# Converting weights two steps ahead in a fused Fourier-mixing and ELU-MLP kernel

## The chip, the cores and the metric

One core of one Trainium2 chip. The metric is the device time of one execution in microseconds (us). All executions quoted are of the fast state. "Before" is the kernel as it was; "the changed kernel" has the change. Most kernels repeat within 0.3% on one chip. Before does not quite: in the sets of the experiments, 48 of its 54 executions took 1976.0 to 1980.9 us and six took 1982.8 to 1987.7. Where another kernel fell in two groups, they are told. "Slow clock" is the time that matmuls lose when TensorE's granted clock has dropped: the trace grants 0.57 of full speed from 112.4 to 115.7 us in before.

## The reference

```python
X = np.fft.fft(np.fft.fft(x, axis=1), axis=2).real.astype(np.float32)      # x: 8 x 3008 x 256, float32
h = X.reshape(24064, 256) @ w_in                        # w_in: 256 x 2048, float64
g = np.where(h > 0, h, np.exp(np.minimum(h, 0)) - 1)
out = (g @ w_out).astype(np.float32)                    # w_out: 2048 x 256, float64
```

Both weights come in as 64-bit floats and are converted on the core, by integer and float work on VectorE, ScalarE and GpSimd.

## The kernel before

TensorE carries the kernel: discrete Fourier transforms as matmuls, the channel transform folded into w_in, then per step of some 5.2 us two blocks of hidden units of one tile of 256 columns. In steps 0 to 15 the first two tiles alternate, so chunk c of w_in (256 hidden units) is first used in step 2c, and chunk c of w_out, which multiplies what came of those hidden units, in step 2c+2. Meanwhile the weights are still being converted. The program gives every piece of work a time on an ideal clock (`T` is one step, 4.8 us on that clock) and emits it in that order; `pin` keeps that order on its engine. What is not pinned, the DMAs above all, a scheduler may move.

```python
# conversion of a chunk: fields (VectorE), power (ScalarE), round and scale (GpSimd, VectorE)
for chunk, k in ((w2_chunks[0], 0), (w1_chunks[2], 1), (w1_chunks[3], 2), (w2_chunks[1], 3),
                 (w1_chunks[4], 4), (w2_chunks[2], 5), ..., (w1_chunks[7], 10),
                 (w2_chunks[5], 11), (w2_chunks[6], 12), (w2_chunks[7], 14)):   # w1 = w_in, w2 = w_out
    ...
# fold of w_in chunk c on TensorE, its copy on ScalarE, its last row to a column by two DMAs
def spread_last_row(q):
    c = slice(q * 256, (q + 1) * 256)
    queue = nc.sync if q else nc.gpsimd
    queue.dma_start(out=wx_dr[:, c], in_=Ws[127:128, c])          # to DRAM
    queue.dma_start(out=wex[:, 2 * q : 2 * q + 2],                 # back as a column
                    in_=wx_dr[:, c].rearrange("o (f p) -> p (o f)", p=128))
# even part on VectorE needs that column:  E = Rb * wex + H
# sums of w_out for later steps, GpSimd
for i in range(8):
    at((11 + 0.7 * i) * T + 1.0, lambda i=i: sum_weights(i))
# loads of one batch of x; two of four go by index, from GpSimd
def load_x(b):
    for j in (2, 1):
        nc.gpsimd.indirect_dma_start(out=L[j], in_=xflat, ...)
    nc.sync.dma_start(out=L[3], ...); nc.sync.dma_start(out=L[0], ...)
    if b == NB - 1:                                                # last batch: one row again
        nc.gpsimd.dma_start(out=L[1][0:1, 0 : 5 * ND], in_=xrows(b, SEQ - 5, 1, 1, 5))
# element-wise loads of one channel of x for all batches (4-byte elements), SyncE
for n in range(16):
    at((13 + 0.7 * n) * T, lambda: load_ext(...))
```

Of the kernel before, what the change touches and what calls it, by code (L numbers as in the profile page):

```python
# [11 lines left out]
U32 = mybir.dt.uint32  # L12
# [5 lines left out]
SEQ = 3008  # L18
ND = 256
NDFF = 2048  # L20
NF = NDFF // 128
HALF = SEQ // 2
# [68 lines left out]
def kernel(  # L91
# [7 lines left out]
    nc = tc.nc  # L99
# [19 lines left out]
    pin = tc.keep_in_program_order  # L119
# [12 lines left out]
    xflat = x.rearrange("b s d -> (b s) d")  # L132
    ix = cpool.tile([128, 3], I32, tag="ix")
# [16 lines left out]
    def load_x(b):  # L150
        L = [
            spool.tile([128, 6 * ND], FP, tag=f"xl{j}", bufs=1, name=f"xl{j}")
            for j in range(4)
        ]
        for j in (2, 1):
            c = 1 if j == 2 else 2 if b == NB - 1 else 0
            nc.gpsimd.indirect_dma_start(
                out=L[j],
                out_offset=None,
                in_=xflat,  # L160
                in_offset=bass.IndirectOffsetOnAxis(
                    ap=ix[:, c : c + 1].bitcast(U32), axis=0
                ),
                element_offset=b * SEQ * ND,
            )
        nc.sync.dma_start(out=L[3], in_=xrows(b, HALF, 6, 128))
        nc.sync.dma_start(out=L[0], in_=xrows(b, 0, 6, 128))
        if b == NB - 1:
            nc.gpsimd.dma_start(
                out=L[1][0:1, 0 : 5 * ND], in_=xrows(b, SEQ - 5, 1, 1, 5)  # L170
            )
        return L
# [5 lines left out]
    Ws = cpool.tile([128, NDFF], FP, tag="Ws")  # L178
# [115 lines left out]
    def w1_dst(c):  # L294
# [6 lines left out]
    IN_HOMES = [(f"WT{c}", 1, 1024) for c in range(4)] + [  # L301
        Wc[:, 1024:2048],
        ("WT0", 1, 1024),
        ("WT1", 1, 1024),
        ("WT2", 1, 1024),
    ]
    OUT_HOMES = [w2[:, 1024 * (c + 1) : 1024 * (c + 2)] for c in range(3)] + [
        ("WT3", 1, 1024),
        ("WT0", 1, 1024),
        ("rx", 1, HALF + 1),  # L310
        ("ot", 2, 1024),
        ("ot", 2, 1024),
# [84 lines left out]
    def fold_chunk(c):  # L397


        ps = folds[c] = bank("H")  # L400
        chunk = w1_chunks[c]
        dst = chunk.dst()
        for n in range(2):
            cols = slice(256 * n, 256 * n + 256)
            for h in range(1 if chunk.pairs else 2):
                for half in range(2):
                    odd = n == half
                    block = 2 * odd + half + 2 * (odd and h)
                    mm(
                        ps[64 * half : 64 * half + 64, cols],  # L410
                        CC[:, 64 * block : 64 * block + 64],
                        chunk.ab[:, 256 * odd : 256 * odd + 256]
                        if chunk.pairs
                        else dst[:, h],
                        n == 0 and h == 0,
                        h == 1 or chunk.pairs,
                    )
# [5 lines left out]

    def spread_last_row(q):
        c = slice(q * 256, (q + 1) * 256)
        queue = nc.sync if q else nc.gpsimd
        queue.dma_start(out=wx_dr[:, c], in_=Ws[127:128, c])
        with nc.allow_non_contiguous_dma(reason="one row to columns"):
            queue.dma_start(
                out=wex[:, 2 * q : 2 * q + 2],  # L430
                in_=wx_dr[:, c].rearrange("o (f p) -> p (o f)", p=128),
            )


    def turn_last_row(q):

        for j in range(2):
            f = 2 * q + j
            mm(
                folds[q][:, j : j + 1],  # L440
                Ws[:, f * 128 : (f + 1) * 128],
                pick[:, 32:33],
                True,
            )

    def put_last_row(q):
        act(wex[:, 2 * q : 2 * q + 2], folds[q][:, 0:2])
# [4 lines left out]
    def sum_weights(i):  # L452
        if not WT:
            for j in range(4):
                WT.append(
                    spool.tile([128, 8, 128], FP, tag=f"WT{j}", bufs=1, name=f"WT{j}")
                )
        b11, b12 = w2v[:, 2 * i, 0:128], w2v[:, 2 * i, 128:256]
        b21, b22 = w2v[:, 2 * i + 1, 0:128], w2v[:, 2 * i + 1, 128:256]
        W = [t[:, i] for t in WT]  # L460
        gtt(W[2], b12, b22, ALU.add)
        gtt(W[1], b11, W[2], ALU.subtract)
        gtt(W[0], b12, b11, ALU.subtract)
        gtt(W[3], W[1], b21, ALU.add)
# [212 lines left out]
    def ext_side(g, rows=NB):  # L677
        n = NO if g > 1 else NE
        t = spool.tile([128, NE], FP, tag="bs", bufs=2, name="bs")
        act(t[0:rows, 0:n], state["ext"][32 * g : 32 * g + rows, 0:n])  # L680
        state["side", g] = t[0:rows, 0:n]
# [392 lines left out]
    def at(t, fn):  # L1074
        events.append((t, len(events), fn))
# [32 lines left out]

    at(-13.1, lambda: dft_now(state["x_even"], 1, "pC"))
    at(-13.1, lambda: dft_now(state["x_even"], 0, "pD"))  # L1110
    at(-13.05, lambda: spread_last_row(0))
    at(-11.5, lambda: state["x_even"].copy())
    at(-11.0, lambda: fold_now("o0 o1 O0 EO2"))
    at(-10.95, R_even.copy)
# [13 lines left out]
    T = PERIOD  # L1128
    for chunk, k in (
        (w2_chunks[0], 0),  # L1130
        (w1_chunks[2], 1),
        (w1_chunks[3], 2),
        (w2_chunks[1], 3),
        (w1_chunks[4], 4),
        (w2_chunks[2], 5),
        (w1_chunks[5], 6),
        (w2_chunks[3], 7),
        (w1_chunks[6], 8),
        (w2_chunks[4], 9),
        (w1_chunks[7], 10),  # L1140
        (w2_chunks[5], 11),
        (w2_chunks[6], 12),
        (w2_chunks[7], 14),
    ):
        t = k * T
        first = (
            (0.96, 0.96, 0.97, 1.9),
            (2.1, 2.9, 2.91, 4.22),
            (2.95, 2.96, 2.97, 4.2),
            (0.95, 0.96, 0.97, 4.2),  # L1150
        )
        dt = first[k] if k < 4 else (-0.5, 0.05, 0.06, 2.95)
        for d, fn in zip(dt, (chunk.fields, chunk.power, chunk.round, chunk.scale)):
            at(t + d, fn)
    for chunk, t in (
        (w1_chunks[6], 0.95),
        (w1_chunks[7], 2.2),
        (w2_chunks[3], 3.2),
        (w2_chunks[4], 7.1),
        (w2_chunks[6], 8.3),  # L1160
        (w2_chunks[7], 12.2),
    ):
        at(t * T, chunk.load)
    for c in range(1, 8):
        t = max(2 * c - 3, c % 3) * T + 4.7 if c > 1 else 2.3
        at(t, lambda c=c: fold_chunk(c))
        t = max(2 * c - 2, 3) * T + 0.03 if c > 1 else 3.0
        at(t, lambda c=c: put_chunk(c))
        if c > 1:
            at(t + 0.01, lambda c=c: spread_last_row(c))  # L1170
    at(3.15, lambda: turn_last_row(1))
    at(T + 0.25, lambda: put_last_row(1))
    for i in range(8):
        at((11 + 0.7 * i) * T + 1.0, lambda i=i: sum_weights(i))
    at(2 * T + 4.2, lambda: fold_now("EO3"))
    total = n_tiles * 8
    WINOGRAD = (
# [75 lines left out]
    def at_half(step, d, par, col):  # L1253
        assert step + 1 >= safe(col)
        t = step * T

        def run():
            d().ps = bank("H")
            d().mms(par, d().ps)

        at(t + 4.75, run)
        if par:
            at(t + T + 1.46, lambda: d().copy())
        else:
            at(t + T + 1.01, lambda: d().plus())
            at(t + T + 1.02, lambda: d().minus())
# [16 lines left out]
    for t, fn in (  # L1283
# [7 lines left out]
        (T + 4.21, R_odd.minus),  # L1291
    ):
        at(t, fn)
    at_half(4, lambda: I_odd, 1, 0)
    at_half(6, lambda: I_odd, 0, HALF)
    at(10 * T + 4.75, dft_ext_0)
    for g in (2, 3):
        at(11 * T + 1.46, lambda g=g: ext_side(g, 1))
    at(12 * T + 1.35, lambda: ext_rows(1, gtt, 1))
    at(12 * T + 2.0, lambda: spread_ext(0, 1))  # L1300
    for n in range(16):
        j, k = divmod(n, 4)
        at(
# [13 lines left out]
    for b in range(1, NB):  # L1317
        s0 = (b - 1) * steps_b
        l0 = s0 - 8 if b > 1 else 5.2
        at(l0 * T + 0.1, lambda b=b: state.update(L=load_x(b)))  # L1320
        f0, f1 = (s0 - 1, s0 + 38) if b > 1 else (8, 37)
        at(f0 * T, lambda b=b: begin_folds(b))
        n = 0
        for key in fold_keys:
            at(
                int(f0 + n * (f1 - f0) / n_big) * T + 1.3,
                lambda key=key: state["ops"][key](),
            )
            n += key[0][0] not in "cx"
        for n, (ri, kodd) in enumerate(((0, 0), (1, 0), (0, 1), (1, 1))):  # L1330
            at_dft(
                s0 + (28, 34, 38, 42)[n], 2, b, ri, kodd,
                lambda k=2 * ri + kodd: state["EO"][k],
            )
        for kodd in range(2):
            step = s0 + (28, 38)[kodd]
            assert step >= safe(b * HALF + (kodd + 1) * RUN)
            at(step * T + 1.0, lambda b=b, kodd=kodd: spread_ext(b, kodd))
# [50 lines left out]
```

## Time and profile before

| | before |
|---|---|
| time, median of the first 3 runs | 1979.11 us (1977.59 to 1979.69) |
| span of the profiled run | 1975.6 us |
| TensorE busy | 1956.9 us |
| waits of TensorE on w_out (steps 4, 10, 12) | 0.95, 1.80, 3.90 us |

TensorE is busy 99% of the span. So the time is its work, plus its idle times, plus what a lowered clock costs after some of them. The prediction shows the lines.

### The profile page before, as it was taken

The page shows a single profiled execution, that of the slowest core. Times are in us where ns is not written, and L with a number is a line of the kernel's source. Part 1 is how long each engine was busy: PE and PEld are TensorE (multiplying, and loading weights), DVE is VectorE, ACT ScalarE, POOL GpSimd, SP SyncE. Part 2 cuts the span into 40 slices and gives each one's busy share as a digit, 9 for nine tenths or more (in the row PEclk, how much of TensorE's full clock was granted, in tenths as well). Part 3 has the DMA queues.
Part 4 walks back from the last instruction along what each step waited for, and adds up shares of the span by engine and source line. Part 5 has one row for each costly group of instructions (what it writes and reads, how often), then busy time and mean ns, then how long its engine had stood idle before and what let it go on. Part 6 is the DMA issues. An engine that isn't in the chain of part 4 may idle for free.

```text
span 1975.6 us, 26860 instructions
## 1 busy us (share of the span) xinstructions
PE 1956.9 (99%) x8908; PEld 1656.1 (84%) x8908; DVE 1275.2 (65%) x2325; ACT 869.0 (44%) x1667; POOL 1361.8 (69%) x1802
## 2 busy tenths in 40 slices
PE   9999999999999999999999999999999999999998
PEld 5778888888888888888888888888888888888887
DVE  8856566666667666666566665666556765666666
ACT  4644434444344444444344443444444444344443
POOL 4678758786587766777567875678657776455665
PEclk9999999999999999999999999999999999999999
DMA  9156101121001110121100211013010110100101
GB/s 354 33 21 88 39 13 19 33 60 24 12 19 43 46 29 11 18 54 37 26 18 13 65 26 26 12 19 89 7 21 11 20 22 14 16 12 12 22 9 24
DMA packets 255610, 71.02 MB, mean 36 GB/s; under 512 B 243998, under 2 KB 244914, under 8 KB 255088
## 3 DMA queue, kind: packets, MB, share of 16 engines
q1 hardware_dynamic: 250896, 56.46, 14.9%
q0 software_dynamic: 2400, 12.59, 1.9%
q8 instruction: 70, 1.15, 0.2%
q14 instruction: 68, 0.56, 0.1%
q10 hardware_dynamic: 2176, 0.26, 0.1%
HBM read 44.43 MB, written 24.80 MB: 35 GB/s over the span
## 4 chain that ended last, share of the span: by engine, by line
PE 96%; DVE 2%; POOL 1%; issue 0%; ACT 0%; POOLq 0%; DVEq 0%
PE H L380 38%; PE pD L380 16%; PE pC L380 16%; PE pB L380 16%; PE pA L380 8%; PE M L380 1%; POOL G L389 0%; DVE E L759 0%; POOL w L389 0%; DVE pow L279 0%; DVE G L785 0%; DVE v L386 0%; DVE pow L225 0%; DVE w L231 0%; DVE Ir L386 0%
## 5 line engine op out<-in xcount | busy, mean ns | idle before, releaser
L389 POOL TENSOR_TENSOR G<-G 128x256 f32<-128x256 f32 x1440 | 1034.7, 728 | 549.2 <-DVE G L785 438.9
L759 DVE SCALAR_TENSOR_TENSOR E<-Rb,wex,H 128x256 f32<-128x256 f32 x752 | 327.9, 477 | 613.0 <-PE H L380 608.1
L392 ACT ACTIVATE G<-H 128x512 f32<-128x512 f32 x376 | 224.5, 597 | 958.6 <-DVE G L769 955.9
L380 PE MATMUL H<-Ir,Ws 128*128 128x256 f32 x1504 | 387.6, 380 | 1.5 <-DVE E L759 1.0
L380 PE MATMUL H<-Rr,Wc 128*128 128x256 f32 x1504 | 387.0, 380 | 0.0
L380 PE MATMUL pC<-G,WT 128*128 128x256 f32 x1440 | 369.6, 379 | 0.0
L380 PEld LDWEIGHTS H<-Rr,Wc 128*128 128x128 f32 x1504 | 284.6, 190 | 56.0 <-issue 4.1
L380 PEld LDWEIGHTS H<-Ir,Ws 128*128 128x128 f32 x1504 | 277.8, 189 | 51.0 <-DVE E L759 3.9
L380 PEld LDWEIGHTS pC<-G,WT 128*128 128x128 f32 x1440 | 273.6, 190 | 37.2
L769 DVE SCALAR_TENSOR_TENSOR G<-E,H 128x512 f32<-128x512 f32 x376 | 257.1, 684 | 44.5 <-PE H L380 8.5
L785 DVE SCALAR_TENSOR_TENSOR G<-G,H 128x512 f32<-128x512 f32 x376 | 255.9, 681 | 24.8 <-ACT G L392 24.8
L785 DVE SCALAR_TENSOR_TENSOR G<-M,G 128x512 f32<-128x512 f32 x376 | 256.9, 683 | 0.0
L380 PE MATMUL pA<-G,w 128*128 128x256 f32 x784 | 231.0, 382 | 6.6 <-POOL w L389 6.6
L392 ACT ACTIVATE G<-G 128x512 f32<-128x512 f32 x376 | 233.3, 620 | 0.0
L380 PE MATMUL pB<-G,w 128*128 128x256 f32 x784 | 229.3, 379 | 0.0
L380 PE MATMUL pD<-G,w 128*128 128x256 f32 x784 | 229.3, 379 | 0.0
L392 ACT ACTIVATE M<-G 128x512 f32<-128x512 f32 x376 | 224.2, 596 | 0.0
L392 ACT ACTIVATE M<-M 128x512 f32<-128x512 f32 x376 | 220.9, 588 | 0.0
L380 PE MATMUL pD<-G,WT 128*128 128x256 f32 x720 | 214.4, 379 | 1.6 <-DVE v L386 1.6
L380 PE MATMUL pB<-G,WT 128*128 128x256 f32 x720 | 214.6, 380 | 0.7 <-POOL G L389 0.6
L380 PEld LDWEIGHTS pA<-G,w 128*128 128x128 f32 x784 | 149.5, 191 | 28.3 <-POOL w L389 7.9
L380 PEld LDWEIGHTS pB<-G,w 128*128 128x128 f32 x784 | 149.0, 190 | 20.2
(137 smaller groups left out, 1401.7 us busy)
## 6 DMA issues: line engine op xcount, KB each, us to landing
out_dram<-ot SPq DMA_DIRECT2D x496, 32.0 KB
xl<-in_x_dram SPq DMA_DIRECT2D x16, 768.0 KB
out_dram<-ot SPq DMA_DIRECT2D x256, 2.0 KB
Rb<-r SPq DMA_DIRECT2D x10, 376.0 KB
raw<-in_moe_w_in_dram SPq DMA_DIRECT2D x7, 512.0 KB
MC<-dft_mats SPq DMA_DIRECT2D x3, 1131.0 KB
raw<-in_moe_w_out_dram SPq DMA_DIRECT2D x5, 512.0 KB
out_dram<-ot SPq DMA_DIRECT2D x64, 28.0 KB
```

The costliest lines, as they stand in the source:

```text
L380: nc.tensor.matmul(out_, lhsT=lhsT, rhs=rhs, start=start, stop=stop, skip_group_check=True)
L389: pin(nc.gpsimd.tensor_tensor(out=o, in0=a, in1=b, op=op))
L392: pin(nc.scalar.activation(out=o, in_=i, func=func, **kw))
L759: nc.vector.scalar_tensor_tensor(out=S.E[:, c], in0=Rb[:, cols(i)], scalar=wex[:, f : f + 1], in1=S.H[:, c], op0=ALU.mult, op1=ALU.add,)
L769: nc.vector.scalar_tensor_tensor(out=two(S.G[:, 0:512])[:, :, ::-1], in0=two(S.E), scalar=2.0, in1=two(S.H), op0=ALU.mult, op1=ALU.subtract,)
L785: nc.vector.scalar_tensor_tensor(out=o, in0=e, scalar=-1.0, in1=h, op0=ALU.add, op1=ALU.max)
```

## The change

The intent: convert every chunk of w_out two steps ahead of its use, in even steps, and w_in in odd ones; put pieces of folding x behind the conversions in GpSimd's order; sum the weights later; make the first weight column with two small matmuls, not two DMAs. Buffers are exchanged to suit. The core of the diff:

```diff
-            nc.gpsimd.indirect_dma_start(
-                out=L[j],
+            pin(
+                nc.gpsimd.indirect_dma_start(
+                    out=L[j],
...
-        queue = nc.sync if q else nc.gpsimd
+        queue = nc.sync
...
-        (w1_chunks[3], 2),
-        (w2_chunks[1], 3),
-        (w1_chunks[4], 4),
-        (w2_chunks[2], 5),
+        (w2_chunks[1], 2),
+        (w1_chunks[3], 3),
+        (w2_chunks[2], 4),
+        (w1_chunks[4], 5),
...                                      # and so on to (w2_chunks[5], 10), (w1_chunks[7], 11)
-        t = max(2 * c - 3, c % 3) * T + 4.7 if c > 1 else 2.3
-        at(t, lambda c=c: fold_chunk(c))
-        t = max(2 * c - 2, 3) * T + 0.03 if c > 1 else 3.0
+        at((2 * c - 2) * T + 4.7 if c > 1 else 2.3, lambda c=c: fold_chunk(c))
+        t = (2 * c - 1) * T + 0.03 if c > 1 else 3.0
...
-    at(-13.05, lambda: spread_last_row(0))
+    at(-10.6, lambda: turn_last_row(0))
+    at(-10.59, lambda: put_last_row(0))
...
-        at((11 + 0.7 * i) * T + 1.0, lambda i=i: sum_weights(i))
+        at((13 + 0.6 * i) * T + 3.6, lambda i=i: sum_weights(i))
...                                      # some transforms one step earlier, homes of chunks
-                int(f0 + n * (f1 - f0) / n_big) * T + 1.3,
+                slot * T + (3.5 if slot < 16 else 1.3),
```

More of the change, by code (lines that the diff above doesn't have):

```diff
@@ L156, in load_x @@
             c = 1 if j == 2 else 2 if b == NB - 1 else 0
-            nc.gpsimd.indirect_dma_start(
-                out=L[j],
-                out_offset=None,
-                in_=xflat,
-                in_offset=bass.IndirectOffsetOnAxis(
-                    ap=ix[:, c : c + 1].bitcast(U32), axis=0
-                ),
-                element_offset=b * SEQ * ND,
+            pin(
+                nc.gpsimd.indirect_dma_start(
+                    out=L[j],
+                    out_offset=None,
+                    in_=xflat,
+                    in_offset=bass.IndirectOffsetOnAxis(
+                        ap=ix[:, c : c + 1].bitcast(U32), axis=0
+                    ),
+                    element_offset=b * SEQ * ND,
+                )
             )
@@ L303 @@
         ("WT0", 1, 1024),
-        ("WT1", 1, 1024),
+        ("WT3", 1, 1024),
         ("WT2", 1, 1024),
@@ L307 @@
     OUT_HOMES = [w2[:, 1024 * (c + 1) : 1024 * (c + 2)] for c in range(3)] + [
-        ("WT3", 1, 1024),
-        ("WT0", 1, 1024),
+        Ws[:, 1024:2048],
+        ("WT1", 1, 1024),
         ("rx", 1, HALF + 1),
@@ L1131 @@
         (w1_chunks[2], 1),
-        (w1_chunks[3], 2),
-        (w2_chunks[1], 3),
-        (w1_chunks[4], 4),
-        (w2_chunks[2], 5),
-        (w1_chunks[5], 6),
-        (w2_chunks[3], 7),
-        (w1_chunks[6], 8),
-        (w2_chunks[4], 9),
-        (w1_chunks[7], 10),
-        (w2_chunks[5], 11),
+        (w2_chunks[1], 2),
+        (w1_chunks[3], 3),
+        (w2_chunks[2], 4),
+        (w1_chunks[4], 5),
+        (w2_chunks[3], 6),
+        (w1_chunks[5], 7),
+        (w2_chunks[4], 8),
+        (w1_chunks[6], 9),
+        (w2_chunks[5], 10),
+        (w1_chunks[7], 11),
         (w2_chunks[6], 12),
@@ L1155 @@
     for chunk, t in (
-        (w1_chunks[6], 0.95),
-        (w1_chunks[7], 2.2),
-        (w2_chunks[3], 3.2),
-        (w2_chunks[4], 7.1),
+        (w2_chunks[3], 0.5),
+        (w2_chunks[4], 0.95),
+        (w1_chunks[7], 3.2),
+        (w1_chunks[6], 5.1),
         (w2_chunks[6], 8.3),
@@ L1293 @@
         at(t, fn)
-    at_half(4, lambda: I_odd, 1, 0)
-    at_half(6, lambda: I_odd, 0, HALF)
-    at(10 * T + 4.75, dft_ext_0)
+    at_half(3, lambda: I_odd, 1, 0)
+    at_half(5, lambda: I_odd, 0, HALF)
+    at(9 * T + 4.75, dft_ext_0)
     for g in (2, 3):
-        at(11 * T + 1.46, lambda g=g: ext_side(g, 1))
-    at(12 * T + 1.35, lambda: ext_rows(1, gtt, 1))
-    at(12 * T + 2.0, lambda: spread_ext(0, 1))
+        at(10 * T + 1.46, lambda g=g: ext_side(g, 1))
+    at(11 * T + 3.55, lambda: ext_rows(1, gtt, 1))
+    at(11 * T + 3.6, lambda: spread_ext(0, 1))
     for n in range(16):
@@ L1324 @@
         for key in fold_keys:
+            slot = int(f0 + n * (f1 - f0) / n_big)
             at(
-                int(f0 + n * (f1 - f0) / n_big) * T + 1.3,
+                slot * T + (3.5 if slot < 16 else 1.3),
                 lambda key=key: state["ops"][key](),
```

## The prediction

> **What bounds the kernel now.** I read the page first (busy shares, chain), then what TensorE waited for, then the timelines of TensorE, GpSimd, VectorE and the DMA queue of SyncE over the first 150 us, since every edited line acts there or only shifts an issue later on.
>
> ```profile
> PE 1956.9 (99%) x8908; PEld 1656.1 (84%) x8908; DVE 1275.2 (65%) x2325; ACT 869.0 (44%) x1667; POOL 1361.8 (69%) x1802
> PE 96%; DVE 2%; POOL 1%; issue 0%; ACT 0%; POOLq 0%; DVEq 0%
> ```
>
> TensorE is busy 1956.9 of 1975.6 us and is 96% of the chain that ended last. So no change that leaves its matmuls alone can win more than the 18.7 us of idle time plus what a lowered clock cost. Of those 18.7 us, 1.1 lie before the first matmul and some 6 after the last one. The rest is a handful of waits (timeline of TensorE: start, us, then in brackets the idle time before and what ended it):
>
> ```profile
> 40.99 1.13 PE L380 MATMUL H<-Ir,Ws 128*128 128x256 f32 x4 [0.95 <-DVE E L759]
> 53.42 1.99 PE L380 MATMUL pA<-G,w 128*128 128x256 f32 x8 [0.95 <-POOL w L389]
> 90.53 1.08 PE L380 MATMUL H<-raw,CC 128*64 128x256 f32 x8 [0.40 <-POOL raw L389]
> 94.47 1.99 PE L380 MATMUL pA<-G,w 128*128 128x256 f32 x8 [1.80 <-POOL w L389]
> 112.40 3.37 PE L380 MATMUL pA<-G,w 128*128 128x256 f32 x8 [3.90 <-POOL w L389]
> 115.56 1.39 PE L380 MATMUL H<-Ir,Ws 128*128 128x256 f32 x4
> 116.78 1.89 PE L380 MATMUL pB<-G,w 128*128 128x256 f32 x8
> ```
>
> The three waits on "POOL w" are matmuls of steps 4, 10 and 12, each the first to need a freshly converted chunk of w_out, whose last multiply GpSimd had not done. The last is the dearest, and slow afterwards: eight matmuls in 3.37 us against 1.89, four in 1.39 against 1.03, so 1.84 us lost to the clock (0.83 granted in the slice from 110 to 120 us). GpSimd shows why it was late:
>
> ```profile
> 102.00 1.29 POOL L389 TENSOR_TENSOR w<-raw,w 128x512 f32<-128x512 f32 x1 [1.75 <-ACT w L392]
> 107.60 0.46 POOL L389 TENSOR_TENSOR WT<-w 128x128 f32<-128x128 f32 x1 [4.31 <-PE H L380]
> ...
> 109.51 1.17 POOL L473 TENSOR_TENSOR e<-xl 128x384 f32<-128x384 f32 x1
> 110.64 1.71 POOL L389 TENSOR_TENSOR w<-w,pow 128x512 f32<-128x512 f32 x1
> ```
>
> The multiply at 110.64 had its operand from VectorE at 104.8. But a weight sum (WT) stood ahead of it in GpSimd's order; its buffer was still the raw home of the last w_in chunk, free only after that chunk's fold matmuls (107.4). Then a fold of x followed. The wait is order, not load.
>
> **What the Trainium skill says.** "TensorE: Matmul & The Clock Gate", first table: the queues of ScalarE, VectorE and GpSimdE are strict FIFO. The trace agrees: 4.31 us of idle GpSimd with a ready multiply behind. The same page, "Why this matters for your kernels": TensorE idle for more than about 3 us falls back to half clock. The trace agrees: after 3.90 us idle, the 1.84 us above; after 1.80 us idle, none. "DMA: Bandwidth & Descriptors", "Queues, rings and completion order": on each DMA engine the descriptors of a ring are consumed in ring order, and SyncE has one row of rings. No wait of before depends on that, but the change will.
>
> **The change part by part.**
> Conversions: w_out chunk c moves from step 2c+1 to step 2c, where its first matmul comes in step 2c+2. In before the multiply ended 5 to 6 us after the first matmul of its step where nothing stood ahead of it (step 5: 59.74 to 64.92; step 7: 73.21 to 79.27). Two steps are at least 10.4 us of TensorE, so the new slack is some 5 us. The three waits go: 0.95+1.80+3.90, and 1.84 of slow clock.
> w_in chunk c moves to step 2c-3 and its fold from step 2c-3 to step 2c-2. The conversion-to-fold distance stays; the x fold pieces that stood before the pairs (84.46 to 87.1) now stand behind, so the 0.40 goes. Sum so far: 0.95+0.40+1.80+3.90+1.84 = 8.9 us.
> First weight column: two more matmuls with one output column (0.36 us in the same job of the next column), and a 0.16 us copy, in place of two DMAs from GpSimd. The VectorE row of step 0 may start 1.6 us earlier (28.61 now), but the one of step 1 waits for matmuls that end 0.36 us later. VectorE is then busy without a gap to 59.7, so the wait of 0.95 at 40.99 stays and swallows both. Zero.
> Later batches: both indirect loads of x become neighbours in GpSimd's order, between the third and fourth sum of a step, with no fold beside them. 2 x 1.02 us delay the fourth sum, which has over 3 us until TensorE uses it (334.6 against 338.0 in a quiet step). No cost; the one wait they caused before (0.59 us at 196.6) goes. Gain 0.6.
> Weight sums: start at step 13.75 instead of 11.2 and must be done in step 18. GpSimd then has some 26 us of work for five steps of 5.2: just enough.
>
> **What it adds: a late column.** The fold of w_in now ends one step before use, not two. Its last row must still go Ws to DRAM to wex by two DMAs on SyncE's queue before VectorE may start the even part of step 2c. When the queue is free this is cheap:
>
> ```profile
> 107.90 0.24 SPq L427 DMA_DIRECT2D wx<-Ws  x1
> 109.03 0.36 SPq L429 DMA_DIRECT2D wex<-wx  x1
> 118.38 0.24 SPq L703 DMA_DIRECT2D r<-rx  x1
> 119.56 0.34 SPq L710 DMA_DIRECT2D Rb<-r  x1
> 119.95 0.29 SPq L714 DMA_DIRECT2D Ir<-r  x1
> 120.28 15.11 SPq L609 DMA_DIRECT2D x<-in_x_dram  x8
> ```
>
> 1.1 us between the two issues, an estimated 2 us to land: about 3.5 in all, against one step of 5.2 us plus 1. It fits for chunks 2 to 6. For chunk 7 it does not. In before its two DMAs preceded the element-wise loads of x. In the built order of the changed kernel SyncE has: the three DMAs of r, one x load, wx of chunk 7, three x loads of 1536 elements, one of 8, then wex of chunk 7. And the even part of step 14 waits for that wex.
> Times: without the old waits the first matmul of step 13 starts at 118.51-8.9 = 109.6, and the last fold is copied 0.5 us later; wx issues at 110.1, just behind the first x load (its row of r is done near 108, plus 1.9 us as from 118.38 to 120.28). Then four x issues and the blocked wx, at 15.11/8 = 1.9 us each, put wex at 110.1+9.5 = 119.6, landed near 121.5. VectorE wants it at 124.75-8.9 = 115.9 (124.75 is that row's start in before). TensorE can go on with one group of eight: its Ir,Ws matmuls of step 14 would start at 114.8+2.6 = 117.4, and start at 121.5+0.9 = 122.4. Idle 5.0 us, and by the rule above a spell of half clock, as after the 3.90: 1.84. New cost 6.8 us.
>
> **Sum.** -8.9-0.6+6.8+0.3 (small waits in steps 7 and 11, where TensorE's step is 5.2 us and VectorE has about 6 us of rows) = -2.4 us, on 1979.1: 1976.7, said as 1976.5.
>
> **The rivals.**
> (a) The column is in time: the x load ahead lets go at once, or the loads are accepted without blocking. For: the first x issue took 0.3 us. Against: eight took 15.11. Then the full 9.5 us comes in at TensorE, but GpSimd, whose weight sums moved later, becomes late at step 18: last w_out chunk's first op near 117, 17 us of ordered work behind it, then three sums, 137.7 against 136.5 wanted, and again once. Costs 1 to 2.5 us: about 1971.5.
> (b) The column lands later still, since small packets ahead drain slowly (the x loads up to 148.7 took over 2 us each), or the clock stays low for longer: 3 to 4 us more, 1980 to 1981. For: 13 x loads in 28 us. Against: only five are ahead.
> (c) GpSimd is the bound throughout the conversions, so that moving work only moves the wait. Against: it has idle times of 1.4 to 3.7 us in nearly every step to 85 us. It would give 1978 to 1979.
>
> **Range and chances.** Most weight on the main line (1974 to 1979), some 20% on (a), 15% on (b). Run to run is 1 us. 80%: 1971 to 1981. Two per cent is 39.6 us, twice all idle time, so faster 0.01; a loss of that size would need a stall in every batch: slower 0.01; within 2% 0.98.
>
> **What would show it.** Right: no "POOL w" before a pA matmul in steps 4, 10, 12; TensorE near 9 us ahead of before at its P matmuls of step 13; then one wait of 4 to 7 us at "H<-Ir,Ws" ended by VectorE's E row near 122 us, that row behind the DMA of wex; a clock under 1 just after; the lead cut to 2 or 3 us. Wrong: no such wait (then (a), and a wait of "pB<-G,WT" on GpSimd near 136), or the wait at 40.99 gone (then the first column was worth something), or any wait on w left.

## The result, and the profile after

| | before | after |
|---|---|---|
| time, median of four runs each | 1978.35 us | 1986.67 us (1985.81 to 1988.87) |
| ratio of the fast runs, 95% interval | | 1.0043 (1.0026 to 1.0060) |
| span of the profiled run | 1975.6 us | 1984.0 us |

A ratio is the mean time of one kernel's fast runs over the mean of the other's in the same rounds, so it is not quite the ratio of the medians. The change made the kernel slower by 0.4%. That is "the same" at 2%, but 8 us, and outside the predicted range.

The page of the changed kernel, busy times and chain:

```profile
PE 1958.9 (99%) x8912; PEld 1658.9 (84%) x8912; DVE 1279.2 (64%) x2325; ACT 869.2 (44%) x1668; POOL 1359.5 (69%) x1800
PE 95%; DVE 2%; DMA 1%; issue 1%; POOL 0%; SPq 0%; ACT 0%; DVEq 0%; POOLq 0%; ACTq 0%
```

The work is that of before. A DMA has come into the chain. In the list of what TensorE waited for, no "POOL w" is left: the three waits of before are gone. Two others, one of 8.43 us and one of 4.12, have come. The timeline of TensorE shows the first (start and duration, us, then in brackets the idle time before and what ended it), in the changed kernel and then at the same places in before:

```profile
110.12 1.13 PE L382 MATMUL H<-Rr,Wc 128*128 128x256 f32 x4
...
116.27 1.89 PE L382 MATMUL pA<-G,w 128*128 128x256 f32 x8
126.58 2.08 PE L382 MATMUL H<-Ir,Ws 128*128 128x256 f32 x4 [8.43 <-DVE E L761]
128.45 3.41 PE L382 MATMUL pB<-G,w 128*128 128x256 f32 x8
```

```profile
118.51 1.03 PE L380 MATMUL H<-Rr,Wc 128*128 128x256 f32 x4
...
126.28 1.03 PE L380 MATMUL H<-Ir,Ws 128*128 128x256 f32 x4
```

The first line of each is the product H<-Rr,Wc of step 13, which the prediction calls its P matmul. TensorE is 8.39 us ahead here. Then it stands idle for 8.43 us in step 14, and the next two groups take 2.08 and 3.41 us in place of 1.03 and 1.89: 2.57 us of slow clock. Together 11.0 us. What it waits for is on VectorE, and behind that in SyncE's queue (DMA issues, SPq):

```profile
125.66 0.87 DVE L761 SCALAR_TENSOR_TENSOR E<-Rb,wex,H 128x256 f32<-128x256 f32 x2 [9.98 <-DMA wex<-wx]
```

```profile
111.13 0.30 SPq L611 DMA_DIRECT2D x<-in_x_dram  x1
112.83 0.62 SPq L429 DMA_DIRECT2D wx<-Ws  x1
113.50 7.34 SPq L611 DMA_DIRECT2D x<-in_x_dram  x4
120.94 0.39 SPq L431 DMA_DIRECT2D wex<-wx  x1
```

The order is the predicted one: four element-wise loads of x stand between the two DMAs of the column. They hold the queue for 7.34 us. The column's second DMA goes at 120.94, and VectorE's row starts when it has landed, at 125.66, 4.7 us later, for one kilobyte.

The second new wait is some 1340 us later, when the last batch is loaded. GpSimd and TensorE of the changed kernel:

```profile
1454.76 0.94 POOL L158 DMA_INDIRECT xl<-in_x_dram,ix  x1 [0.30 <-issue]
1461.72 0.53 POOL L171 DMA_DIRECT2D xl<-in_x_dram  x1 [6.03 <-DMA xl<-in_x_dram,ix]
```

```profile
1463.08 1.22 PE L382 MATMUL pD<-G,w 128*128 128x256 f32 x2 [4.12 <-POOL G L391]
1464.09 1.91 PE L382 MATMUL H<-Rr,Wc 128*128 128x256 f32 x4
```

The one-row load writes into a tile that the indirect load is still writing, so it must wait for it. GpSimd's sums stand behind it, and TensorE behind those: 4.12 us idle and 0.63 + 0.88 us of slow clock (the two groups take 0.59 and 1.03 at full clock) and 0.18 in the next, 5.8 in all. In before the scheduler had moved both loads some 80 us ahead and put other work between the two, and the wait was 0.53:

```profile
1373.15 0.96 POOL L157 DMA_INDIRECT xl<-in_x_dram,ix  x1 [0.27 <-DVE G L785]
...
1378.64 0.54 POOL L169 DMA_DIRECT2D xl<-in_x_dram  x1 [0.53 <-DMA xl<-in_x_dram,ix]
```

The two traces add up: -8.4 (the lead at step 13) + 11.0 + 5.8 = +8.4, and the spans differ by 8.4.

### The profile page after: what moved, and what is told of

It is laid out like the page before. It is cut to its first block, busy times and chain, and to the rows that moved or that the text cites. A ratio compares the mean times of both kernels' runs of the same rounds, so it can differ in the third digit from the quotient of the medians.

```text
span 1984.0 us, 26864 instructions
## 1 busy us (share of the span) xinstructions
PE 1958.9 (99%) x8912; PEld 1658.9 (84%) x8912; DVE 1279.2 (64%) x2325; ACT 869.2 (44%) x1668; POOL 1359.5 (69%) x1800
## 4 chain that ended last, share of the span: by engine, by line
PE 95%; DVE 2%; DMA 1%; issue 1%; POOL 0%; SPq 0%; ACT 0%; DVEq 0%; POOLq 0%; ACTq 0%
PE H L382 38%; PE pB L382 16%; PE pD L382 16%; PE pC L382 16%; PE pA L382 8%; DMA xl<-in_x_dram,ix 1%; DVE E L761 0%; SPq L611 0%; DVE e L475 0%; DVE pow L281 0%; POOL G L391 0%; DMA wex<-wx 0%; DVE G L787 0%; DVE v L388 0%; DVE u L388 0%
## 5 line engine op out<-in xcount | busy, mean ns | idle before, releaser
L382 PEld LDWEIGHTS pD<-G,w 128*128 128x128 f32 x784 | 149.1, 190 | 24.7 <-POOL G L391 4.5
```

Source lines behind the costliest of these rows:

```text
L382: nc.tensor.matmul(out_, lhsT=lhsT, rhs=rhs, start=start, stop=stop, skip_group_check=True)
```

## The experiments

The theory: the change wins some 9 us in the conversions, and gives back 11 because the last column stands behind loads of x (theory 1), and 5.8 because the pinned indirect loads bring the one-row load right behind them (1b). The rivals: GpSimd, now with its weight sums later, is what costs (2); the neighbouring indirect loads cost in every batch (2b); or slower DMAs from the start, run to run (3). Eleven kernels ran in twelve sets, all correct.

| kernel | median, us | ratio to before (95%) |
|---|---|---|
| the changed kernel | 1986.67 | 1.0043 (1.0026 to 1.0060) |
| a_order | 1993.03 | 1.0067 (1.0053 to 1.0081) |
| e_turn7 | 1976.16 | 0.9990 (0.9976 to 1.0004) |
| b_row_sync | 1982.35 | 1.0021 (1.0007 to 1.0035) |
| g_turn7_row | 1970.38 | 0.9963 (0.9949 to 0.9977) |
| i_scalar_q | 1983.12 | 1.0026 (1.0010 to 1.0041) |
| k_copy_first | 1988.15 | 1.0041 (1.0029 to 1.0052) |
| f_before_pin | 1983.33 | 1.0022 (1.0008 to 1.0037) |
| d_before_sums_later | 1977.72 | 0.9998 (0.9978 to 1.0018) |
| d_again (same kernel) | 1974.19 | 0.9985 (0.9973 to 0.9997) |
| l_before_col | 1979.06 | 1.0007 (0.9989 to 1.0025) |
| m_g_fold_early | 1970.33 | 0.9948 (0.9929 to 0.9968) |
| j_best | 1968.44 | 0.9938 (0.9918 to 0.9958) |

The median of before in these sets was 1977.83 to 1978.09 us. Rows a, e, b, g ran on one chip; i, d, f, l on another; k, m, j and, in a set of its own, d_again on a third. The ratios are of means, so slow executions of before in a set (one in that of i, d, f, l, four in that of k, m, j) lower them: by medians j_best is at 0.9951, not 0.9938, and f at 1.0028. A difference of 0.001 between rows of different sets is within that.

**The last column without the queue: e_turn7.**

```diff
         if c > 1:
-            at(t + 0.01, lambda c=c: spread_last_row(c))
+            if c < 7:
+                at(t + 0.01, lambda c=c: spread_last_row(c))
...
+    at(13 * T + 2.2, lambda: turn_last_row(7))
+    at(13 * T + 2.9, lambda: put_last_row(7))
```

> The changed kernel, but the two columns of the last w_in chunk are made by TensorE (two matmuls with one output column, one copy), as the change does for the first chunk, in place of two DMAs. Theory 1: the wait of step 14 goes by another way than the order of a queue: 11.0 less, 0.4 more for the two matmuls, about 1976.1. Theory 2: less than 3 us won. If the wait were in the Ws copy or the fold and not in the DMAs, this kernel keeps most of it (over 5 us at the same place).

Measured 1976.16, 10.5 less than the changed kernel where 10.6 was expected. The wait of step 14 is gone and the 1b wait is there (4.45 us). So theory 1 holds with its size, and theories 2 and 3 fall as causes of this wait. Behind the wait two smaller ones came to light, of which TensorE's timeline of this kernel shows the first; the second, of 0.57 us, is at 145.51:

```profile
139.92 0.70 PE L382 MATMUL pB<-G,WT 128*128 128x256 f32 x2 [1.14 <-POOL G L391]
```

That is the lateness of GpSimd after the weight sums, which the prediction's rival (a) put at 1 to 2.5 us: 1.7 here. The long wait had hidden it.

**The same by order: a_order.**

```diff
-        queue.dma_start(out=wx_dr[:, c], in_=Ws[127:128, c])
+        pin(queue.dma_start(out=wx_dr[:, c], in_=Ws[127:128, c]))
...                                  # pin also round the wex DMA and every load of x
-            (13 + 0.7 * n) * T,
+            (13.1 + 0.7 * n) * T,
```

> The changed kernel, but the element-wise loads of x on SyncE are kept behind the two DMAs of the last weight column (order kept for both, loads of x timed 0.1 step later); nothing else. Theory 1 (the column of chunk 7 stands behind loads of x in SyncE's queue): the wait of 8.43 us at the Ir,Ws matmuls of step 14 and the slow clock after it (2.57) go: 11.0 us less than the changed kernel, about 1975.7, with the wex DMA issued near 114 us and landed before 117.2. Theory 2 (the later weight sums and the piled-up work of GpSimd cost the time): the wait moves to the weight sums or stays elsewhere, less than 3 us won, about 1984 to 1986. Theory 3 (slower DMAs from the start, run to run): no change, 1986.7.

Slower than the changed kernel. The wait of step 14 is indeed gone: the E row of step 14 (VectorE's even part) started at 116.80, waiting for a matmul and no DMA.

```profile
114.30 0.38 SPq L431 DMA_DIRECT2D wex<-wx  x1
```

```profile
116.80 0.87 DVE L762 SCALAR_TENSOR_TENSOR E<-Rb,wex,H 128x256 f32<-128x256 f32 x2 [0.76 <-PE H L382]
```

With the loads of x behind it in the queue, the column's second DMA was in place at most 2.5 us after its issue. But pinning every load of x strung the later ones out between output stores. The whole channel of x arrived late, in TensorE's timeline:

```profile
191.00 4.17 PE L382 MATMUL H<-MC,xe 128*8 128x377 f32 x24 [13.66 <-POOL xe L391]
```

So 13.66 us of idle time, with slow clock after it, for the 8.43. The edit did two things, and the time judges their sum; the trace tells them apart. It also shows that these loads of x have a deadline of their own.

**Order or landing: i_scalar_q.**

```diff
-        queue = nc.sync
+        queue = nc.scalar if q == 7 else nc.sync
```

> The changed kernel, but the two DMAs of the last weight column are issued from ScalarE's queue, right behind the copy of that row, and the loads of x stay where they are on SyncE: the order of all other instructions is the same. If the whole delay is the order of SyncE's queue (blocked loads of x ahead of wex), wex is issued near 115 and lands within some 2 us, before the 117.2 at which VectorE's row must start: the wait of 8.43 and its slow clock go, 11.0 less, about 1975.7. If loads of x in flight make the small DMA land late whatever its queue (it took 4.7 us from issue to landing in the changed kernel, against an estimated 2), it lands near 120 and 2 to 3 us of wait stay: about 1979. The first run of this kind (order kept on SyncE) took the wait away and was yet 6 us slower than the changed kernel, since its later loads of x came between output stores; this one leaves those alone, so a loss here would speak against that reading.

Between the two: 1983.12, and in the ratio 0.0017, some 3.4 us, below the changed kernel. The two intervals overlap, so the trace has to decide. No load of x stands ahead of the column on this queue. Issues from ScalarE, VectorE's row, TensorE, and the share of DMA time from 108 to 126 us (packets, MB, share of 16 engines; q1 is SyncE's queue):

```profile
112.04 0.49 ACTq L429 DMA_DIRECT2D wx<-Ws  x1
116.40 0.39 ACTq L431 DMA_DIRECT2D wex<-wx  x1
```

```profile
122.09 0.87 DVE L761 SCALAR_TENSOR_TENSOR E<-Rb,wex,H 128x256 f32<-128x256 f32 x2 [7.68 <-DMA wex<-wx]
```

```profile
123.02 2.07 PE L382 MATMUL H<-Ir,Ws 128*128 128x256 f32 x4 [5.69 <-DVE E L761]
```

```profile
q1 hardware_dynamic: 9200, 0.47, 80.8%
```

Each of the two one-kilobyte DMAs took long from issue to landing: 4.36 us and 5.69. With the queue free the first took 1.1 us (107.90 to 109.03 in before, which the prediction shows). The 9200 packets of x loads were in flight on SyncE's queue and filled four fifths of the DMA engines' time. The Trainium skill says why the landing need not get better on another queue ("DMA: Bandwidth & Descriptors", "Issuing engines are not separate DMA queues"): DMAs from any engine run on the same 16 DMA engines and interleave. The trace agrees: on ScalarE's queue the second DMA took 5.69 us, and in a_order, issued ahead of the loads of x, at most 2.5. So the wait has two parts, the order of the queue and the landing behind x. When only the first is taken away, 5.69 of 8.43 us stay.

**The copy ahead: k_copy_first.**

```diff
+        f = 4.1 if c == 7 else 4.7          # fold of chunk 7 timed ahead of the activations
+        t = 12 * T + 4.15 if c == 7 else t  # and so its copy
```

> The changed kernel, but ScalarE copies the last folded chunk (Ws, Wc) ahead of the four activations of step 12 rather than behind them; the order of all other engines is the same. This tests the term of 2.7 us by which the first DMA of the last column was issued later than predicted (112.83 against 110.1). If ScalarE's order is that term, wx is issued near 111, wex some 1.8 us earlier, and the wait of 8.43 at step 14 becomes 6.6: 1.8 less than the changed kernel, about 1984.9. If loads of x already blocked set when wex goes, less than 0.5 us is won. What stays of the wait is then the blocked loads and the late landing.

No gain: ratio 1.0041 against 1.0043. SyncE's issues and TensorE in this kernel:

```profile
110.82 1.97 SPq L429 DMA_DIRECT2D wx<-Ws  x1
...
120.37 0.39 SPq L431 DMA_DIRECT2D wex<-wx  x1
```

```profile
125.96 2.07 PE L382 MATMUL H<-Ir,Ws 128*128 128x256 f32 x4 [8.53 <-DVE E L761]
```

The first DMA was issued 2.0 us earlier, but its own issue was then blocked for 1.97 us in place of 0.62, and the second went at 120.37. In both kernels the next load of x is issued 2.4 us after the first one (110.42 to 112.83 here, 111.13 to 113.50 there), so the first load of x paces the queue. The second DMA gained 0.57 us, so the late copy in the changed kernel cost at most that, and nothing that shows in the times.

**The one-row load: b_row_sync and f_before_pin.**

```diff
         if b == NB - 1:                 # b_row_sync, in the changed kernel
-            nc.gpsimd.dma_start(
+            nc.sync.dma_start(
```

> The changed kernel, but the one-row load of the last batch goes by SyncE's queue, not GpSimd's; the order of all other instructions is the same. Theory 1b (that load, now right behind its indirect load in GpSimd's order, makes GpSimd wait 6.03 us near 1461 us): TensorE's wait of 4.12 us there and some 1.5 us of slow clock go: 5.6 us less, about 1981.1, with the wait of step 14 still there. Theory 2b (the neighbouring indirect loads themselves cost in every batch): at most 0.6 us won, since nothing else of the batches is altered.

```diff
-            nc.gpsimd.indirect_dma_start(...)      # f_before_pin, in the kernel before
+            pin(nc.gpsimd.indirect_dma_start(...))
```

> The kernel before with its indirect loads of x kept in program order on GpSimd, as the change has them, nothing else. If the pin alone makes the one-row load of the last batch follow its indirect load and block GpSimd, a wait of some 4 us at pD near 1454 us with slow clock after it: 5.6 us more than before; the wait of 0.59 at 196.6 may go: 1983.0 to 1983.7. If the blocking needs the rest of the change: no difference, 1978.

Taking it away from the changed kernel: 1982.35, in the ratio 0.0022, some 4.3 us less. Putting the pin alone into before: 1983.33, 0.0022 more. By medians the two are 4.3 and 5.5 us, where 5.6 was expected: the same in both directions, to about 1 us. (The profile of b is of its quickest execution, 1977.49, the others took 1979.5 to 1983.2; part of that is luck with the clock, 1.61 us lost after a wait of 8.36 at step 14.) In b TensorE's longest wait for GpSimd is 0.5 us. In f it is there at once (GpSimd, TensorE):

```profile
1459.84 0.54 POOL L169 DMA_DIRECT2D xl<-in_x_dram  x1 [6.40 <-DMA xl<-in_x_dram,ix]
```

```profile
1461.19 1.22 PE L380 MATMUL pD<-G,w 128*128 128x256 f32 x2 [4.50 <-POOL G L389]
```

So 1b is shown and 2b falls: the other batches, whose indirect loads are neighbours too but have no row load behind them, show no such wait (the changed kernel has one wait of pD on GpSimd, f one). The wait near 196 us stayed (0.50 us at 197.39 in f, 0.49 at 199.32 in the changed kernel). The prediction had it gone.

**Both: g_turn7_row.** The edits of e_turn7 and b_row_sync together.

> Both of the two preceding edits. If the two new waits are all that the change cost, they add: 11.0+5.6-0.4 = 16.2 us less than the changed kernel, about 1970.5, and 7.9 us less than the kernel before, which is the lead of 8.4 us that the trace of the changed kernel shows at step 13. If a further wait comes up behind them (weight sums at step 16 to 18, GpSimd late as in the prediction's rival a), 1 to 3 us more: 1971.5 to 1973.5, with a pB or pC wait on GpSimd near 135 us.

1970.38: 16.3 less than the changed kernel in the medians, 15.8 in the ratios, 16.2 expected. The longest wait of TensorE left in this kernel (us in total, times, longest):

```profile
PE pB L382 <- POOL G L391: 2.2, 3, 1.1
```

With two stalls removed the change is worth 0.37% against before. This is the gain that the moved conversions and sums had made all along; of it, the later sums alone give some 4 us in their quick executions (d, next).

**Only the weight sums: d_before_sums_later and d_again.**

```diff
-        at((11 + 0.7 * i) * T + 1.0, lambda i=i: sum_weights(i))     # in the kernel before
+        at((12 + 0.7 * i) * T + 1.0, lambda i=i: sum_weights(i))
```

> The kernel before with the weight sums one step later (start at step 12.2 in place of 11.2), nothing else of the change. If the wait of 3.90 us at step 12 was only the order on GpSimd (a weight sum, waiting for its buffer, ahead of a ready multiply), it and the slow clock after it (1.84) go: 5.7 us less than before, about 1972.4, with the waits of steps 4 and 10 (0.95, 1.80) still there. If GpSimd had too much to do in these steps, the wait moves to step 14 or to the weight sums near step 16, and it is within 1 us of before, about 1978.

> The kernel before with the weight sums one step later, once more, on whatever chip comes: its first six runs fell in two groups (1972.6 to 1974.4, and 1981.1 to 1981.6), and its profile was of the quick group (span 1971.5, no wait at step 12, a new wait of 1.82 us for GpSimd at 141.95). If the quick group is what the edit gives and the other was a disturbance of that chip, most runs are near 1973 to 1974 here, 4 to 5 less than before. If the two groups are the kernel's own, both come again, and a profile of the slow one would show a wait or a slow clock of 7 to 8 us that the other lacks.

The first set fell in two groups, three runs at 1972.6 to 1974.4 and three at 1981.1 to 1981.6; the second gave nine at 1972.5 to 1975.6 and three at 1981.1 to 1983.7. In both profiles the wait of 3.90 at step 12 is gone, so it was order alone, as the prediction reasoned. The second profile caught the slow group (span 1979.5, the first 1971.5). TensorE in the second:

```profile
142.95 0.70 PE L380 MATMUL pB<-G,WT 128*128 128x256 f32 x2 [1.88 <-POOL G L389]
143.48 1.76 PE L380 MATMUL H<-Ir,Ws 128*128 128x256 f32 x4
...
184.82 3.75 PE L380 MATMUL H<-MC,xe 128*8 128x377 f32 x24 [3.66 <-POOL xe L389]
```

In the first profile the wait for GpSimd is nearly the same (1.82), but the next group takes 1.03 in place of 1.76, and the matmuls of xe there (178.41) do not wait. So the slow executions carry a slow clock after 1.88 us idle, and 3.66 us for the channel of x, the deadline that a_order had shown. The loads themselves ran slower there: SyncE's first eight loads of x held its queue for 19.85 us from 119.26, against 15.15 from 118.33 in the first profile. What slowed them is not known. Two profiles are two executions; that every slow one is so is likely, not shown.

**Two small parts: l_before_col and m_g_fold_early.**

```diff
-    at(-13.05, lambda: spread_last_row(0))       # l_before_col, in the kernel before
+    at(-10.6, lambda: turn_last_row(0))
+    at(-10.59, lambda: put_last_row(0))
```

> The kernel before with the first weight column made by TensorE, as the change has it, in place of two DMAs from GpSimd. The prediction put it at zero (VectorE busy without a gap up to the wait at step 2, which stays): within 0.5 us of before. If the column DMAs had delayed the start, or the conversions on GpSimd, up to 1.6 us less.

```diff
-                slot * T + (3.5 if slot < 16 else 1.3),    # m_g_fold_early, in g_turn7_row
+                slot * T + 1.3,
```

> The version of 1970.4 with the fold pieces of x put back ahead of the conversions on GpSimd (each 1.3 us into its step, as in the kernel before, not 3.5). The prediction gave this part of the change 0.40 us (a fold waiting for pairs at 90.5). If it is worth that: 0.4 to 1 us more, about 1971, with a wait of H on raw near 88 us. If the conversions two steps ahead already have the slack, no difference.

The first column by TensorE is worth nothing that shows: 1.0007, with an interval of about 1.8 per thousand to either side, and the wait at step 2 stays (1.12 us at 41.01). Fold pieces ahead of the conversions: 1970.33, where the version with them behind had 1970.38 on another chip. The expected wait on raw near 88 us did not come; one of 0.96 us on VectorE's E row at 105.33 did, against 0.21 in g_turn7_row, too little to see in the time. That part of the change is inconclusive under 1 us.

**A further version: j_best.** Two more edits on g_turn7_row.

```diff
-            (2.1, 2.9, 2.91, 4.22),
+            (2.1, 2.9, 2.91, 5.8),          # a multiply of w_in chunk 2 behind the E row of step 2
...
+            if b == 1 and 14 <= slot < 28:  # fold pieces of steps 14 to 18 later, sums first
+                slot = 19 + (slot - 14) * 9 // 14
```

> The best version so far (last column by TensorE, one-row load on SyncE; 1970.4) with two more edits: the weight sums go ahead of the fold pieces of x in steps 14 to 18 on GpSimd (the pieces are spread over steps 19 to 27), and the last multiply of w_in chunk 2's conversion on VectorE goes behind the even part of step 2. If the waits left at pB in steps 16 and 17 (1.14 and 0.57) and at step 2 (1.11) each go at no cost elsewhere: 2.8 less, about 1967.6. If GpSimd is only late later (1.5 pieces a step where 1 fitted) or the fold of chunk 2 is late by 0.9, within 1 us of 1970.4.

1968.44, or 1.9 less than m_g_fold_early on the same chip, and 0.62% under before (0.49% by medians): the quickest kernel of this study. The waits at pB in steps 16 and 17 went, and one of 0.75 came at 151.46. The one at step 2 only changed its name: it is now the fold of chunk 2 that waits, for the multiply that was put back. And the channel of x, at 174.71, is late by 0.97 us.

```profile
42.78 1.08 PE L382 MATMUL H<-raw,CC 128*64 128x256 f32 x8 [1.08 <-POOL raw L391]
```

## Why the prediction was wrong, point by point

**Right: what goes.** The three waits on w, the slow clock after the last and the fold's wait went. The lead at step 13 was predicted at 8.9 and is 8.39 in a run whose first transform of the even part of x ("pA<-MC,e") began 0.67 us later than in before (20.60 against 19.93): 9.06 without that. Its cause, a weight sum ahead of a ready multiply, is shown by d for the largest of them. The wait at step 2 stayed, and the first column was worth zero (l).

**Right in mechanism, wrong in size: the late column.** The text had the queue's order, the E row that waits, and the issue of wex: 119.6 predicted, 120.94 found, 1.3 late. The term that failed is "an estimated 2 us to land": the sum took 1.9, and 4.7 were measured. The prediction names no source for it, and the landing that it shows (wx in at most 1.1 us) is of a free queue; it was used in a stretch where element-wise loads were in flight. VectorE came free when predicted (115.68 against 115.9), though the matmul that its row also needs ended only at 116.43, and TensorE reached the wait at 118.15 where 117.4 was predicted. So the idle time was 8.43 in place of 5.0 (2.8 from the landing, 1.3 from the issue, less the 0.75 by which TensorE came later), with 2.57 of slow clock in place of 1.84: 11.0 for 6.8. The slow clock is partly chance: after nearly the same idle time it cost 1.61 in b_row_sync and 2.14 in k_copy_first. i_scalar_q shows the landing apart from the order. Rival (b), small packets ahead draining slowly and 3 to 4 us more, was the right one, and had been given 15%. It alone would have kept the time near 1981, at the edge of the range.

**Missed, and what took the time out of the range: "No cost" for the later batches.** The text reckoned the two issues of the indirect loads and not what stands behind them in the last batch: a load into the same tile, which has to wait for the indirect load to land, and now follows it at once. 5.8 us in the trace, 4.3 to 5.5 in the times (b, f). Added alone to the predicted 1976.7 it gives 1982.5. The one small wait that this step had counted as gone stayed (0.49).

**The sum again.** 1976.7 + 4.2 (column) + 5.8 (row) + 0.5 (wait that stayed) + 0.2 (a lead of 8.39 where 8.9 less 0.3 was reckoned) = 1987.4. The median of before was 1978.35 and not the 1979.1 that the prediction started from, which makes it 1986.65; measured 1986.67. The four runs lie 3 us apart, so agreement to better than 1 us is luck. "Run to run is 1 us" was too small as well: see the executions of before, above.

**Rival (a)**, GpSimd late after the weight sums, was real too, 1.7 us, but hidden under the long wait until e_turn7 removed it. **Rival (c)** falls: the waits on w went.

## What to carry to other kernels

A wait found in an engine's order is won by reordering; then follow the work that now has less slack, down to the DMAs, and price those with the queue and the DMA engines as full as they will be at that moment. When an instruction is pinned or moved, look at the one that now stands right behind it and ask what it must wait for: here one line for one batch cost half or more of what ten moved conversions had won (4.3 to 5.8 of 8.4 us). Waits hide behind one another, so remove the largest first and read the trace again.

## What the Trainium skill lacked or had wrong

- "TensorE: Matmul & The Clock Gate", "Why this matters for your kernels", gives gaps over about 3 us as what drops the clock. The runs show slow spells after shorter ones, in some executions and not in others: after 1.80 us idle eight matmuls took 3.47 us in f_before_pin (clock 0.55) and 1.99 in before (clock 1.00); after 1.88 and 1.82 the next four took 1.76 and 1.03 in the two profiles of one kernel. So here a gap under 2 us was followed by a slow spell in some executions.
- "DMA: Bandwidth & Descriptors", "Latency and other measured facts", gives some 2 us as the fixed cost of a DMA. It has no figure for a small DMA issued among element-wise loads: one kilobyte took 4.4 to 5.7 us here, while packets nearly all of 4 bytes held 81 to 86% of the engines' time, and at most 2.5 us in a_order, where it went ahead of those loads.
- No page tells what a load costs that follows an indirect load into the same tile on GpSimd: it held GpSimd for 6.03 and 6.40 us.
